# Streaming the attention prologue: normalising and projecting chunk by chunk inside the attention loop, with row statistics moved beside the residual adds

## The chip, the cores and the metric

The kernel runs on 1 core of one Trainium2 chip. The metric is the device time of one execution in microseconds (us). Executions of one kernel on one chip lie within about 0.3% of each other; a time more than 1.5% above the fastest of the same kernel counts as slow and is left out of comparisons.

Engines are named as in the profile: PE is TensorE (matmul), PEld its weight loads, DVE is VectorE, ACT is ScalarE, POOL is GpSimd, SP is SyncE.

## The reference

A sequence of 2048 rows of 512 features goes through four layers: attention (A), gated MLP (B), A, B, each on a layer-normalised copy and added back to the residual.

```python
def _A_ref(x, wq, wk, wv, wo):            # 32 heads of 16, one shared K and V
    q = (x @ wq).reshape(B, S, H, Dh).transpose(0, 2, 1, 3)
    k = x @ wk
    v = x @ wv
    p = softmax(einsum('bhqd,bkd->bhqk', q, k) * Dh ** -0.5)
    return einsum('bhqk,bkd->bhqd', p, v).transpose(0, 2, 1, 3).reshape(B, S, H * Dh) @ wo

def _B_ref(x, w_in, w_sp, b_sp, w_out):
    z = gelu(x @ w_in)
    z1, z2 = z[..., :Fh], layernorm(z[..., Fh:])
    g = einsum('ts,bsf->btf', w_sp, z2) + b_sp[None, :, None]
    return (z1 * g) @ w_out

x = x + A(layernorm(x)); x = x + B(layernorm(x))
x = x + A(layernorm(x)); x = x + B(layernorm(x))
```

## The kernel before

The kernel emits one instruction stream per engine; `K.op(engine, fn, waits, inc)` appends an operation with the semaphore values it waits for. Each stream is executed in the order in which it was appended, so a wait at its head holds up everything behind it (DVE's 5.32 us of idle time before L235, in the timeline of layer 0 below, is such a wait).

Every layer begins with this normalisation of all 16 row tiles (128 rows each):

```python
def layer_norm_T(lst, x_waits, extra_pe_waits):
    for t in range(NT):                                   # 16 statistics
        v = K.op("dve", ... e.bn_stats(ln_stats[:, t, :], X[:, t, :]), waits=x_waits, inc=S_dloc)
    v_stats = v
    for t in range(NT):
        v = K.op("dve", ... e.bn_aggr(ln_mv[:, t, :], ln_stats[:, t:t + 1, :]), waits=[(S_dloc, v_stats)], inc=S_dve)
    v1 = K.op("act", ... e.activation(ln_veps[:], ln_mv[:, :, 1], ACTF.Sqrt, bias=eps_c[:, 0:1]), ...)
    v_rstd_v = K.op("dve", ... e.reciprocal(ln_rstd[:], ln_veps[:]), waits=[(S_act, v1)], inc=S_dve)
    for t in range(NT):
        v = K.op("dve", ... e.tensor_scalar(xn[:, t, :], X[:, t, :], mean, rstd, subtract, mult), ...)
    # ... 8 groups: PE transposes two tiles into a PSUM bank, DVE copies them to xnT
```

Attention then makes K for all 4 chunks of 512 rows, V for all, and two of the 32 (chunk, head group) blocks of Q, and only then starts its loop:

```python
kT_ready = (S_dve, v_k_last)        # all of K
V_ready = (S_dve, v_v_last)         # all of V
...
emit_fill(0); emit_fill(1)          # scores of 3 blocks each, into PSUM
for i in range(NI):                 # 683 turns
    emit_exp(i)                     # ACT: exponential of 128 x 1536
    for u in pending_pv.get(i, []):
        emit_pv(u)                  # PE: probabilities times V
        emit_acc(u)                 # DVE: accumulate out of PSUM
    if i + 2 < NI:
        emit_fill(i + 2)            # PE: scores for two turns later; waits for exponential i
    emit_side_pe(allow_bg=(i % SIDE_PERIOD == 0))   # one "side task" on PE: Q block, ...
    emit_side_dve()                                 # and its copy on DVE
```

Side tasks share one PSUM bank (bank 7); each waits until the copy of the task before has emptied it. The six banks of scores, one of the accumulation and this one are the eight PSUM banks that the kernel addresses.

The softmax here doesn't subtract the row's maximum and nothing guards it: scores larger than these inputs give would overflow.

## Time and profile before

| | before |
|---|---|
| median of the first 5 executions | 2643.57 us (2641.64 to 2651.72) |
| ACT busy | 79% of the span |
| first exponential of layer 0 | 58.2 us |
| last residual add of layer 1 to first exponential of layer 2 | 36.1 us |

From the page of the kernel before: the busy line of all engines, then two rows of the 40 equal slices of the span (a digit is a tenth of busy time, or of the full TensorE clock), then the group of the exponentials with its count, busy time, mean ns and idle time.

```profile
PE 1924.7 (73%) x11232; PEld 541.8 (20%) x11232; DVE 1219.6 (46%) x2035; ACT 2081.7 (79%) x1653; POOL 0.7 (0%) x7
...
ACT  1999999999999999272029999999999999973800
...
PEclk9985555555555555698989555555555555557899
...
L669 ACT ACTIVATE P_ring<-ps_all 128x1536 bf16<-128x1536 f32 (+1 forms) x1366 | 1907.2, 1450 | 124.2 <-PE ps_all L650 92.3
```

ACT is at 9 in the two attention layers and below that only around the layer changes. The clock row says 5 (half of full speed) in most of attention.

From the timeline of the same run, the prologue of layer 0 (start, duration, engine, line, operation; in brackets the idle time before it and what ended it):

```profile
19.92 1.09 DVE L235 TENSOR_SCALAR w_out_r<-w_out_r 128x3584 bf16<-128x3584 bf16 x1 [5.32 <-DMA w_out_r<-in_B_w_out_dram]
...
22.74 8.97 DVE L254 BATCH_NORM_STATS2 ln_stats<-X 128x6 f32<-128x512 bf16 x15
31.75 1.17 DVE L258 BATCH_NORM_AGGREGATE ln_mv<-ln_stats 128x2 f32<-128x6 f32 x16
32.95 0.31 ACT L261 ACTIVATE ln_veps<-ln_mv,eps_c 128x16 f32<-128x16 f32 x1 [30.94 <-DVE ln_mv L258]
...
33.29 0.25 DVE L263 RECIPROCAL ln_rstd<-ln_veps 128x16 f32<-128x16 f32 x1 [0.37 <-ACT ln_veps L261]
33.58 5.25 DVE L267 TENSOR_SCALAR xn<-X,ln_mv,ln_rstd 128x512 bf16<-128x512 bf16 x16
...
45.87 3.73 PE L332 MATMUL ps_all<-xnT,wk_rep 128*128 128x512 bf16 x16 [0.79 <-DVE xnT L293]
...
58.20 2.79 ACT L669 ACTIVATE P_ring<-ps_all 128x1536 bf16<-128x1536 f32 x2 [23.64 <-PE ps_all L650]
```

All of this is serial: 16 statistics until 31.7 us, aggregation, the square root on ACT and reciprocal on DVE, 16 normalises, transposes, K, V, Q. ACT waits 23.6 us for the first scores. From the timeline around the change from layer 1 to layer 2:

```profile
1332.77 0.69 DVE L968 TENSOR_TENSOR X<-ps_all,X 128x512 bf16<-128x512 f32 x1 [0.82 <-PE ps_all L962]
1333.50 9.59 DVE L254 BATCH_NORM_STATS2 ln_stats<-X 128x6 f32<-128x512 bf16 x16
1343.12 1.17 DVE L258 BATCH_NORM_AGGREGATE ln_mv<-ln_stats 128x2 f32<-128x6 f32 x16
...
1369.58 2.79 ACT L669 ACTIVATE P_ring<-ps_all 128x1536 bf16<-128x1536 f32 x2 [23.65 <-PE ps_all L650]
```

Last residual add, 9.6 us of statistics, and the first exponential 36.1 us after the add ended (1369.58 - 1333.46).

The windows view of a stretch in the middle of attention (length, then busy us and instruction count for each engine, then the granted clock):

```profile
core 0: us, PE busy (x) PEld busy (x) DVE busy (x) ACT busy (x) POOL busy (x), PEclk, DMA share, GB/s
398.00:458.00 60.00, 43.63 (x262) 9.13 (x258) 23.29 (x36) 58.37 (x43) 0.00 (x0) 0.50 0.00 1
```

### The profile page before, as it was taken

What the parts mean: (1) busy time and instruction counts of PE and PEld (TensorE: products, weight loads), DVE (VectorE), ACT (ScalarE), POOL (GpSimd) and SP (SyncE); (2) the same over time, 40 slices, a digit from 0 to 9 for tenths busy, and PEclk for the clock granted to TensorE, in tenths of its full rate; (3) what the DMA queues carried; (4) which work ended last, traced back from release to release, by engine and by line L of the source; (5) the groups of instructions that cost most, each with busy time, mean ns of one, the idle gap of its engine ahead of it and who ended that gap; (6) DMA issues with size and microseconds to landing.
All of it is one profiled execution on the core that took longest, in us unless ns stands there. A gap on an engine that the chain in (4) does not pass through costs nothing.

```text
span 2642.8 us, 29476 instructions
## 1 busy us (share of the span) xinstructions
PE 1924.7 (73%) x11232; PEld 541.8 (20%) x11232; DVE 1219.6 (46%) x2035; ACT 2081.7 (79%) x1653; POOL 0.7 (0%) x7
## 2 busy tenths in 40 slices
PE   3888777777777777568968777777777777765699
PEld 2232111111111111223432111111111111112144
DVE  5655433343334333792366334333433343339733
ACT  1999999999999999272029999999999999973800
POOL 0000000000000000000000000000000000000000
PEclk9985555555555555698989555555555555557899
DMA  3053000000000000201000000000000000001020
GB/s 114 1 139 101 1 0 1 0 1 1 1 1 1 1 1 1 64 0 32 32 1 1 0 1 1 0 1 0 1 1 1 1 1 1 1 1 64 0 67 30
DMA packets 60042, 44.00 MB, mean 17 GB/s; under 512 B 34816, under 2 KB 57216, under 8 KB 59904
## 3 DMA queue, kind: packets, MB, share of 16 engines
q1 hardware_dynamic: 59904, 42.11, 5.4%
q8 instruction: 92, 1.51, 0.2%
q14 instruction: 46, 0.38, 0.0%
HBM read 31.62 MB, written 10.49 MB: 16 GB/s over the span
## 4 chain that ended last, share of the span: by engine, by line
PE 42%; DVE 27%; ACT 23%; issue 7%; DMA 0%; SPq 0%; ACTq 0%
ACT P_ring L669 21%; PE ps_all L684 21%; DVE acc_sb L707 13%; PE ps_all L930 7%; PE ps_all L650 7%; DVE ybuf L832 2%; PE ps_all L962 2%; PE ps_all L613 2%; DVE st L858 2%; DVE ln_stats L254 1%; DVE z2n L853 1%; DVE oT_bf L709 1%; ACT z2n L886 1%; DVE z1c L853 1%; PE ps_all L561 1%
## 5 line engine op out<-in xcount | busy, mean ns | idle before, releaser
L669 ACT ACTIVATE P_ring<-ps_all 128x1536 bf16<-128x1536 f32 (+1 forms) x1366 | 1907.2, 1450 | 124.2 <-PE ps_all L650 92.3
L707 DVE TENSOR_TENSOR acc_sb<-ps_all,acc_sb 128x512 f32<-128x512 f32 x896 | 618.4, 690 | 928.3 <-PE ps_all L684 926.8
L684 PE MATMUL ps_all<-P_ring,V_aug 128*32 128x512 bf16 x4096 | 600.7, 574 | 472.4 <-ACT P_ring L669 257.4
L650 PE MATMUL ps_all<-qT_pad,kT_rep 32*128 32x512 bf16 x4096 | 783.7, 572 | 25.0 <-ACT P_ring L669 12.1
L684 PEld LDWEIGHTS ps_all<-P_ring,V_aug 128*32 128x32 bf16 x4096 | 129.3, 100 | 937.5 <-ACT P_ring L669 914.1
L650 PEld LDWEIGHTS ps_all<-qT_pad,kT_rep 32*128 32x128 bf16 x4096 | 141.3, 97 | 584.4 <-issue 421.3
L930 PE MATMUL ps_all<-wspT,z2n 128*128 128x512 bf16 x896 | 209.1, 390 | 24.3 <-ACT z2n L886 24.3
L261 ACT ACTIVATE ln_veps<-ln_mv,eps_c 128x16 f32<-128x16 f32 x4 | 1.2, 308 | 223.1 <-DVE ln_mv L258 223.1
L930 PEld LDWEIGHTS ps_all<-wspT,z2n 128*128 128x128 bf16 x896 | 88.3, 99 | 144.1 <-ACT z2n L886 27.5
L843 ACT ACTIVATE thbuf<-ybuf 128x448 bf16<-128x448 f32 (+1 forms) x120 | 72.2, 601 | 55.0 <-DVE ybuf L832 51.0
L940 DVE TENSOR_TENSOR gtmp<-ps_all,bsp_bc 128x512 f32<-128x512 f32 x56 | 38.7, 692 | 151.0 <-PE ps_all L930 151.0
L785 PE MATMUL ps_all<-w_in_r,xnT 128*128 128x448 bf16 x256 | 67.0, 394 | 44.7 <-DVE z2n L853 42.8
L283 PE MATMUL ps_all<-ident,xn 128*128 128x128 bf16 x256 | 29.6, 310 | 86.7 <-DVE xn L267 73.4
L823 ACT ACTIVATE ybuf<-ps_all 128x448 f32<-128x448 f32 (+1 forms) x120 | 66.3, 553 | 28.1 <-PE ps_all L785 27.6
L832 DVE SCALAR_TENSOR_TENSOR ybuf<-ybuf,ps_all 128x448 f32<-128x448 f32 (+1 forms) x120 | 75.4, 628 | 3.5 <-ACT ybuf L823 3.2
L709 DVE TENSOR_TENSOR oT_bf<-ps_all,acc_sb 128x512 bf16<-128x512 f32 x64 | 44.2, 691 | 70.4 <-PE ps_all L684 70.3
L790 PE MATMUL ps_all<-xnT,w_in_r 128*128 128x512 bf16 x224 | 62.6, 408 | 10.8 <-DVE z1c L853 9.3
L408 DVE CAST qT_pad<-ps_all 128x512 bf16<-128x512 f32 x60 | 41.5, 692 | 50.6 <-PE ps_all L403 50.6
L403 PE MATMUL ps_all<-xnT,wq_pad 128*128 128x512 bf16 x240 | 62.2, 382 | 0.3 <-DVE o_norm L571 0.3
L962 PE MATMUL ps_all<-w_out_r,hT 128*128 128x512 bf16 x224 | 49.7, 379 | 12.1 <-DVE hT L946 12.1
L613 PE MATMUL ps_all<-wo_r,onT 128*128 128x512 bf16 x128 | 44.7, 486 | 10.2 <-DVE X L618 6.6
L561 PE MATMUL ps_all<-ident,oT_bf 128*128 128x128 bf16 x256 | 37.7, 299 | 19.5 <-DVE oT_bf L709 19.5
(62 smaller groups left out, 726.7 us busy)
## 6 DMA issues: line engine op xcount, KB each, us to landing
wspT<-wspt_scratch SPq DMA_DIRECT2D x8, 2048.0 KB, 8.2
wsp_stage<-in_B_w_sp_dram SPq DMA_DIRECT2D x16, 512.0 KB, 3.9
wspt_scratch<-wspT_tile SPq DMA_DIRECT2D x16, 512.0 KB, 5.0
X<-in_A_x_dram SPq DMA_DIRECT2D x1, 2048.0 KB, 8.4
out_dram<-X SPq DMA_DIRECT2D x16, 128.0 KB, 3.4
w_in_r<-in_B_w_in_dram SPq DMA_DIRECT2D x1, 1792.0 KB, 9.4
w_out_r<-in_B_w_out_dram SPq DMA_DIRECT2D x1, 896.0 KB, 10.6
wq_nat<-in_A_wq_dram SPq DMA_DIRECT2D x1, 512.0 KB, 9.5
```

What stands on the lines that cost most here:

```text
L613: ins = e.matmul(side_bank32[:, 0:D], onT[:, par, c, qt * 128:(qt + 1) * 128], wo_r[:, c, :], start=(c == 0), stop=(c == 3))
L650: ins = e.matmul(bk[:, 0:QC], kT_rep[32 * j:32 * j + 32, kt * 128:(kt + 1) * 128], qT_pad[32 * j:32 * j + 32, hg, qc * QC:(qc + 1) * QC], ...
L669: return e.activation(P_ring[:, s0:s0 + n, :], bank32(b0, n).rearrange("p (k q) -> p k q", k=n)[:, :, 0:QC], ACTF.Exp, scale=DH ** -0.5)
L684: ins = e.matmul(pv_bank[32 * j:32 * j + 32, 0:QC], V_aug[:, kt, 32 * j:32 * j + 32], P_ring[:, slot, :], tile_position=(0, 32 * j), start ...
L707: fn = lambda e: e.tensor_tensor(acc_sb[:], pv_bank[:, 0:QC], acc_sb[:], ALU.add)
L709: fn = lambda e: e.tensor_tensor(oT_bf[:, par, :], pv_bank[:, 0:QC], acc_sb[:], ALU.add)
L785: ins = e.matmul(bk[:, 0:448], xnT[:, kd, t * 128:(t + 1) * 128], w_in_r[:, kd, FH + h * 448:FH + (h + 1) * 448], start=(kd == 0), stop=(k ...
L823: st["a0"][k] = K.op("act", lambda e, slot=slot, bk=bk, n=n: e.activation(ybuf[:, slot, 0:n], bk[:, 0:n], ACTF.Square, scale=SQA), waits=w ...
L832: st["d3"][k] = K.op("dve", lambda e, slot=slot, bk=bk, n=n: e.scalar_tensor_tensor(ybuf[:, slot, 0:n], ybuf[:, slot, 0:n], GELU_C, bk[:, ...
L843: st["a1"][k] = K.op("act", lambda e, slot=slot, n=n: e.activation(thbuf[:, slot, 0:n], ybuf[:, slot, 0:n], ACTF.Tanh), waits=wl, inc=S_act)
L930: ins = e.matmul(bk[:, 0:TCW], z2n[:, sti, ft * 128:(ft + 1) * 128], wspT[:, wb, sti, :], start=(sti == 0), stop=(sti == NT - 1))
L962: ins = e.matmul(bk[:, 0:D], hT2[:, ft, tt * 128:(tt + 1) * 128], w_out_r[:, ft, :], start=(ft == 0), stop=(ft == NF1 - 1))
```

## The change

The intent is to let the exponentials start sooner. Three things are done:

1. The row statistics (`bn_stats`) leave the head of each layer. Each tile's are computed just after its residual add: in attention by DVE in a turn of the loop that has nothing urgent, in layer 1's output beside the matmuls of the next tile.
2. Attention normalises, transposes and projects only chunk 0 of 4 ahead of its loop. Chunks 1 to 3 become urgent side tasks (normalise, two transpose groups, K, V each). The scores of a key tile wait only for their own chunk.
3. The reciprocal root of the attention layers moves from ACT and DVE to POOL (add, then power -0.5), and 10 (layer 0) or 18 (layer 2) dummy matmuls on PE run meanwhile, the "warm-up" matmuls (`pe_warm` in the code). They are meant to bring PE to its full clock.

```diff
+    def ln_rstd_tiles(t0, n, v_mv):
+        v1 = K.op("pool", lambda e: e.tensor_scalar(ln_veps[:, t0:t0 + n], ln_mv[:, t0:t0 + n, 1], LN_EPS, None, op0=ALU.add),
+                  waits=[(S_dve, v_mv)], inc=S_ploc)
+        v2 = K.op("pool", lambda e: e.tensor_tensor(ln_rstd[:, t0:t0 + n], ln_veps[:, t0:t0 + n],
+                                                     mhalf[:, 0:1].to_broadcast([P, n]), ALU.pow),
+                  waits=[(S_ploc, v1)], inc=S_pool)
...
     def layer_norm_T(lst, x_waits, extra_pe_waits):
-            v = K.op("dve", lambda e, t=t: e.bn_stats(ln_stats[:, t, :], X[:, t, :]),
-                     waits=list(x_waits) + [(S_dloc, None)], inc=S_dloc)
...
     def layer_A(layer_idx, x_waits, do_wspt=False):
-        xn, xnT, xnT_v = layer_norm_T(lst, x_waits, extra_pe_waits=[])
-        xnT_all = (S_dve, max(xnT_v))
+        if layer_idx == 0:
+            for t in range(NT):
+                v_st = K.op("dve", lambda e, t=t: e.bn_stats(ln_stats[:, t, :], X[:, t, :]), waits=list(x_waits), inc=S_dloc)
+        for t in range(NT):
+            v_mv = K.op("dve", lambda e, t=t: e.bn_aggr(ln_mv[:, t, :], ln_stats[:, t:t + 1, :]), ...)
+        rstd_w = ln_rstd_tiles(0, NT, v_mv)
+        def pe_warm(e, n=10 if layer_idx == 0 else 18):
+            for _ in range(n):
+                ins = e.matmul(bank32(3)[:, 0:512], ident[:], wo_r[:, 0, :], start=True, stop=True)
+            return ins
+        K.op("pe", pe_warm, ...)
+        v_x0, _ = ln_direct_chunk(0, x_waits, xn, XR, xnT, [0, 1], bfree, rstd_w=rstd_w)
...  # K, V of chunk 0 and two Q blocks only
+        for c in range(1, NCH):
+            t_lns = make_lns_task(c)
+            side_urgent.append(t_lns)
+            for half in range(nh):
+                side_urgent.append(make_lnt_task(c, half))
+            side_urgent.append(make_k_task(c))
+            side_urgent.append(make_v_task(c))
...
         def emit_fill(i):
-                while (qc, hg) not in qT_ready:
+                kc = kt // CT
+                while (qc, hg) not in qT_ready or kc not in kT_ready:
                     progressed = emit_side_pe()
...
             emit_side_dve()
+            if st_pending and not side_urgent and i % 8 == 5:
+                emit_stat()
...
     # layer_B, after each residual add
+                if layer_idx == 1:
+                    vx = K.op("dve", lambda e, t=t: e.bn_stats(ln_stats[:, t, :], X[:, t, :]), waits=[(S_dve, vx)], inc=S_dve)
```

## The prediction

> **What bounds it now.** Two attention layers and two gated-MLP layers run in turn. In attention the exponential on ScalarE sets the pace: in 60 us windows ScalarE is busy 58 to 59.5 us, one 128x1536 exponential each 1.36 us (33.73 us for 25, granted clock 1.0) to 1.43 us (30.14 us for 21, clock 0.5). The change leaves that alone. Serial prologues stand between the layers (timeline view):
> - layer 0: row statistics end at 31.7 us, first exponential 58.2;
> - layer 2: last residual add ends 1333.5, first exponential 1369.6: 36 us;
> - layers 1 and 3: 9.6 us of statistics each (1070.1 and 2377.4), VectorE alone.
>
> **Removed from the critical path** (durations of the trace, scheduled by hand)
> - Statistics move beside the residual adds: in attention into VectorE slack (23 of 60 us busy), in the MLP output beside 1.5 us of matmuls per tile. Only the last tile's 0.65 us stays: 9.0 us saved in each of layers 1 and 3 and in layer 2.
> - Only chunk 0 of 4 is normalised, transposed and projected before attention. From aggregation start to first exponential: 1.2 aggregation + about 1 reciprocal root on GpSimd (estimate from its 0.1 to 0.3 us operations plus handoffs) + 0.7 + 0.7 slack for the warm-up matmuls + 2.7 transposes and copies + 3.9 K, V, Q0, Q1 on TensorE + 0.75 last copy + 0.5 scores = 11.6 us. Layer 0's first exponential comes near 43.3 us: 15 saved. Layer 2: 36.1 becomes about 12.3: 24 saved, its statistics included.
> - Sum: 15 + 24 + 18 = 57 us.
>
> **Added on the path.** Chunks 1 to 3 (12 normalises of 0.33, 6 transposes groups of 0.95, 3 K and 3 V of 0.9 to 1.07, and a 0.4 to 0.7 us copy each) go into the first 16 or so exponentials of each attention. There VectorE and TensorE each need about 1.5 us per exponential, against 1.36. Worse, the scores of key tile 4, 8, 12 wait for their chunk's transpose, copy, K, copy chain on in-order queues. By hand: a stall of about 2.5 us before exponential 5, 1 to 1.5 at the next two boundaries, 0.3 to 0.5 at some others: 7 us per attention, 14 in all. Statistics delaying an accumulation: about 1 us.
>
> **The warm-up matmuls** (10 and 18). The Trainium skill, "TensorE: Matmul & The Clock Gate", Part 1, says that the idle array runs at half clock until some 3.4 us of activity. The trace agrees in layer 2 (granted clock 0.50 from 1337 to 1353 us, then 1.00), but shows 1.00 throughout layer 0's prologue, and transposes cost 0.115 us at either. I expect under 2 us from them, of either sign.
>
> **Prediction: 57 - 15 = 42 us less: 2602 us** (-1.6%), 80% range 2588 to 2616. Chances: over 2% faster 0.13, within 2% 0.86, over 2% slower 0.01.
>
> **What would show it.** First exponential at 42 to 45 us; in layer 2 about 12 us after the last residual add; the MLP layers go from last residual add to aggregation in under 1 us; in the first 25 us of each attention ScalarE idles some 7 us, released by the scores, most before its sixth exponential; the steady attention at 1.43 us as before, with granted clock 0.5.
>
> **What would make it wrong.** GpSimd's power taking several us (it is on both attention prologues); stalls of the streamed chunks hiding (gain up to 52) or a cold array doubling them (gain under 30); moved statistics delaying accumulation at each tile; a different clock in attention, where 0.07 us per exponential over 1366 would be 100 us.

## The result, and the profile after

The changed kernel takes 2608.18 us (median of 9 executions, 2603.18 to 2963.03), the kernel before 2643.57 us (15 executions). The ratio of fast runs is 0.9859, with a 95% interval of 0.9846 to 0.9872: 1.4% faster, within the 2% band that counts as the same. Ratios are the mean time of one kernel's fast runs over that of the other's in the same rounds, so they are not quite the ratio of the medians quoted.

The execution that was profiled first took 2963 us, in the slow state. Its trace holds no clock record at all, and the profile prints a clock of 1.00 for it. Its matmuls tell another story. From the timeline of its layer 0:

```profile
32.19 4.83 PE L400 MATMUL ps_all<-wo_r,ident 128*128 128x512 bf16 x10 [32.19 <-DVE ln_stats L392]
...
40.17 1.95 PE L411 MATMUL ps_all<-xnTA,wk_rep 128*128 128x512 bf16 x4 [0.79 <-DVE xnTA L287]
```

Ten 128x512 matmuls in 4.83 us, and the K of one chunk (4 matmuls) in 1.95 us, where before had 16 such in 3.73 us including waits: here it ran at about half clock. The mean 128x512 matmul of layer B's largest group took 674 ns against 390 before. It was not at one low clock throughout, though: in steady attention (exponentials 171 to 341 of layer 0) the median score matmul took 506 ns, between the 602 ns of the second profile below (granted clock 0.50 there) and the 384 ns of e11 (1.00). It is not compared further. All readings of "after" below are from a second profile of the same kernel (2604.76 us median of 4 executions on its chip, ratio 0.9858).

The lines of the page that answer to those of before:

```profile
PE 1905.3 (73%) x11198; PEld 538.0 (21%) x11260; DVE 1220.9 (47%) x2033; ACT 2081.1 (80%) x1650; POOL 7.1 (0%) x11
...
ACT  2999999999999999373049999999999999974800
...
PEclk9986555555555555698999655555555555557899
...
L809 ACT ACTIVATE P_ring<-ps_all 128x1536 bf16<-128x1536 f32 (+1 forms) x1366 | 1908.8, 1451 | 272.5 <-PE ps_all L790 242.5
```

ACT's idle time before exponentials is not to be compared as it stands: ACT no longer does a square root in the gap between layers 1 and 2, so the gap of 139.1 us, which `before` books under that root, is now booked under the exponentials. The timeline of layer 0's prologue:

```profile
31.91 1.17 DVE L394 BATCH_NORM_AGGREGATE ln_mv<-ln_stats 128x2 f32<-128x6 f32 x16
...
32.02 4.22 PE L400 MATMUL ps_all<-wo_r,ident 128*128 128x512 bf16 x10 [32.02 <-DVE ln_stats L392]
...
33.17 0.26 POOL L258 TENSOR_SCALAR ln_veps<-ln_mv 128x16 f32<-128x16 f32 x1 [31.66 <-DVE ln_mv L394]
...
33.51 2.93 POOL L260 TENSOR_TENSOR ln_rstd<-ln_veps,mhalf 128x16 f32<-128x16 f32 x1
...
36.48 1.38 DVE L268 TENSOR_SCALAR xnA<-X,ln_mv,ln_rstd 128x512 bf16<-128x512 bf16 x4 [3.40 <-POOL ln_rstd L260]
...
45.84 2.79 ACT L809 ACTIVATE P_ring<-ps_all 128x1536 bf16<-128x1536 f32 x2 [43.85 <-PE ps_all L790]
```

First exponential at 45.8 us instead of 58.2. The reciprocal root is the longest item: 0.26 us of add and 2.93 us of power on POOL, 3.40 us with the handoffs, where before had 0.66. Then the change from layer 1 to layer 2:

```profile
1319.67 0.69 DVE L1122 BATCH_NORM_STATS2 ln_stats<-X 128x6 f32<-128x512 bf16 x1
1320.40 1.17 DVE L394 BATCH_NORM_AGGREGATE ln_mv<-ln_stats 128x2 f32<-128x6 f32 x16
...
1332.69 2.79 ACT L809 ACTIVATE P_ring<-ps_all 128x1536 bf16<-128x1536 f32 x2 [139.06 <-PE ps_all L790]
```

From the end of the last residual add (1319.64) to the first exponential: 13.1 us instead of 36.1. And the change from layer 0 to layer 1, last residual add, one statistic, aggregation:

```profile
1064.29 0.69 DVE L755 TENSOR_TENSOR X<-ps_all,X 128x512 bf16<-128x512 f32 x1 [1.25 <-PE ps_all L750]
1065.01 0.69 DVE L560 BATCH_NORM_STATS2 ln_stats<-X 128x6 f32<-128x512 bf16 x1
1065.74 1.17 DVE L318 BATCH_NORM_AGGREGATE ln_mv<-ln_stats 128x2 f32<-128x6 f32 x16
```

Only one tile's statistics are left between add and aggregation, 0.76 us instead of 9.66. Last, the new stall of the streamed chunks, before exponential 5 (counting from 0) of layer 0:

```profile
51.24 1.03 PE L279 MATMUL ps_all<-ident,xnA 128*128 128x128 bf16 x8
...
52.31 0.69 DVE L287 COPY xnTA<-ps_all 128x1024 bf16<-128x1024 bf16 x1 [0.77 <-PE ps_all L279]
...
53.06 1.04 PE L411 MATMUL ps_all<-xnTA,wk_rep 128*128 128x512 bf16 x3 [0.24 <-DVE xnTA L287]
54.13 0.69 DVE L416 CAST kT_rep<-ps_all 128x512 bf16<-128x512 f32 x1 [0.53 <-PE ps_all L411]
...
54.88 0.39 PE L790 MATMUL ps_all<-qT_pad,kT_rep 32*128 32x512 bf16 x3 [0.79 <-DVE kT_rep L416]
...
55.32 2.79 ACT L809 ACTIVATE P_ring<-ps_all 128x1536 bf16<-128x1536 f32 x2 [2.52 <-PE ps_all L790]
```

Transpose, copy, K, copy, scores: each waits for the one before, on in-order queues, and ACT idles 2.52 us at the end of it.

The gain, place by place, from the starts of the same operations in the two traces:

| place | before, us | after, us | gain, us |
|---|---|---|---|
| layer 0: first exponential | 58.20 | 45.84 | 12.4 |
| layer 0: first exponential to end of the last | 994.1 | 1001.4 | -7.3 |
| layer 1: last add of layer 0 to aggregation | 9.66 | 0.76 | 8.9 |
| layer 2: last add of layer 1 to first exponential | 36.1 | 13.1 | 23.1 |
| layer 2: first exponential to end of the last | 990.0 | 997.0 | -7.0 |
| layer 3: last add of layer 2 to aggregation | 9.66 | 0.76 | 8.9 |
| rest of layers 1 and 3 | | | -0.9 |
| sum | | | 38.1 |

In both attention layers, 6.1 of the 7 us given back are lost in the first 32 exponentials; the rest of attention has nearly the same intervals, turn by turn, as before.

### The profile page after: what moved, and what is told of

It is laid out like the page before. It is cut to its first block, busy times and chain, and to the rows that moved or that the text cites. A ratio compares the mean times of both kernels' runs of the same rounds, so it can differ in the third digit from the quotient of the medians.

```text
span 2961.1 us, 29539 instructions
## 1 busy us (share of the span) xinstructions
PE 2269.8 (77%) x11260; PEld 603.8 (20%) x11260; DVE 1225.2 (41%) x2033; ACT 2059.4 (70%) x1650; POOL 7.1 (0%) x11
## 4 chain that ended last, share of the span: by engine, by line
PE 57%; DVE 21%; ACT 16%; issue 5%; DMA 0%; SPq 0%; POOL 0%; ACTq 0%
PE ps_all L829 19%; ACT P_ring L809 15%; PE ps_all L1080 14%; DVE acc_sb L852 12%; PE ps_all L790 7%; PE ps_all L513 4%; PE ps_all L940 4%; PE ps_all L1112 4%; PE ps_all L750 2%; DVE st L1008 1%; DVE oT_bf L854 1%; ACT z2n L1036 1%; DVE z2n L1003 1%; DVE ybuf L982 1%; PE ps_all L698 1%
## 5 line engine op out<-in xcount | busy, mean ns | idle before, releaser
L809 ACT ACTIVATE P_ring<-ps_all 128x1536 bf16<-128x1536 f32 (+1 forms) x1366 | 1884.3, 1452 | 483.5 <-PE ps_all L790 475.3
L829 PE MATMUL ps_all<-P_ring,V_aug 128*32 128x512 bf16 x4096 | 576.2, 555 | 523.2 <-ACT P_ring L809 260.0
L790 PE MATMUL ps_all<-qT_pad,kT_rep 32*128 32x512 bf16 x4096 | 706.1, 521 | 26.6 <-DVE kT_rep L416 3.3
L1080 PE MATMUL ps_all<-wspT,z2n 128*128 128x512 bf16 x896 | 421.9, 674 | 25.1 <-ACT z2n L1036 25.1
L1080 PEld LDWEIGHTS ps_all<-wspT,z2n 128*128 128x128 bf16 x896 | 132.0, 148 | 314.2 <-issue 286.4
L513 PE MATMUL ps_all<-xnTA,wq_pad 128*128 128x512 bf16 x240 | 117.1, 649 | 0.7 <-DVE o_norm L708 0.7
L1112 PE MATMUL ps_all<-w_out_r,hT 128*128 128x512 bf16 x224 | 104.6, 674 | 12.1 <-DVE hT L1096 12.1
L935 PE MATMUL ps_all<-w_in_r,xnT 128*128 128x448 bf16 x256 | 106.9, 567 | 8.8 <-DVE z2n L1003 6.3
L940 PE MATMUL ps_all<-xnT,w_in_r 128*128 128x512 bf16 x224 | 104.8, 678 | 0.6 <-DVE z2n L1003 0.6
L698 PE MATMUL ps_all<-ident,oT_bf 128*128 128x128 bf16 x256 | 32.5, 275 | 24.8 <-DVE oT_bf L854 24.8
L1112 PEld LDWEIGHTS ps_all<-w_out_r,hT 128*128 128x128 bf16 x224 | 32.3, 147 | 84.4 <-issue 63.7
```

Of the source, the lines that this page charges most:

```text
L513: ins = e.matmul(side_bank32[:, 0:QC], wq_pad[:, kd, hg, :], xnT[:, kd, qc * QC:(qc + 1) * QC], start=(kd == 0), stop=(kd == KD - 1))
L790: ins = e.matmul(bk[:, 0:QC], kT_rep[32 * j:32 * j + 32, kt * 128:(kt + 1) * 128], qT_pad[32 * j:32 * j + 32, hg, qc * QC:(qc + 1) * QC], ...
L809: return e.activation(P_ring[:, s0:s0 + n, :], bank32(b0, n).rearrange("p (k q) -> p k q", k=n)[:, :, 0:QC], ACTF.Exp, scale=DH ** -0.5)
L829: ins = e.matmul(pv_bank[32 * j:32 * j + 32, 0:QC], V_aug[:, kt, 32 * j:32 * j + 32], P_ring[:, slot, :], tile_position=(0, 32 * j), start ...
L935: ins = e.matmul(bk[:, 0:448], xnT[:, kd, t * 128:(t + 1) * 128], w_in_r[:, kd, FH + h * 448:FH + (h + 1) * 448], start=(kd == 0), stop=(k ...
L940: ins = e.matmul(bk[:, 0:TCW], w_in_r[:, kd, ft * 128:(ft + 1) * 128], xnT[:, kd, tc * TCW:(tc + 1) * TCW], start=(kd == 0), stop=(kd == K ...
```

## The experiments

Four kernels ran on one chip with a kernel before of 2643.15 us, four on another with 2649.09, four on a third with 2641.35. All twelve gave correct results. The first of them (e1) is the changed kernel itself, whose profile has just been shown.

> The changed kernel again, unaltered, because its profile on record fell in a slow execution. Expected: about 2608 us in the fast state. In the profile: first exponential of layer 0 near 46 us (the slow profile had 49.1 with cold matmuls; aggregation ends 33.2, the root on GpSimd takes 0.26 + 2.93 us instead of the 1 us in the prediction), layer 2's first exponential 14 to 15 us after its last residual add. Theory A (the shortfall of 37 measured against 42 predicted is GpSimd's power, 2 x 2.4 us): exponential stalls in the first 25 us of each attention sum to about 7 us. Rival B (the shortfall is the streamed chunks): those stalls sum to 10 us or more per attention. Rival C (the moved statistics delay accumulations): steady attention per head group is longer than the 30.63 us of before.

**Measured.** 2604.76 us, ratio 0.9858 (0.9844 to 0.9871). First exponential of layer 0 at 45.8, of layer 2 13.1 us after the add. ACT's idle time before exponentials 1 to 17 sums to 5.1 us in each attention. Rival B wanted 10 or more, theory A about 7. Theory A's account of the shortfall, two slow roots, is taken up under e5: it holds only in part. Rival C, longer head groups everywhere, does not hold: apart from one spot near exponential 512 (+1.4 and +1.8 us) and stretches in layer 0 where the clock changes, the intervals are those of before.

### e2: the statistics alone

```diff
# on the kernel before
-            v = K.op("dve", ... e.bn_stats(ln_stats[:, t, :], X[:, t, :]) ...)   # head of layers 1, 2, 3
+            # emit_stat() in attention and bn_stats after layer 1's residual adds, as in the change
```

> The kernel before with only the row statistics moved beside the residual adds. Theory A: the statistics leave the critical path whole, all but the last tile's: 3 x 9.0 = 27 us less than before, near 2617 us (ratio 0.990). Rival C (the moved statistics delay accumulations in attention or the residual chain of the MLP): 20 us or less.

**Measured.** 2619.0 us, ratio 0.9908 (0.9894 to 0.9923): 24 us less than before. Last residual add to aggregation is 0.76 us in all three places, so 3 x 8.9 = 26.7 us left the path as expected; 1 to 4 us were lost again inside attention. That is nearer to theory A (27) than to rival C (20 or less), though the interval of the ratio, 20 to 28 us, does not separate the two; the trace does.

### e3: the streaming alone

```diff
# on the changed kernel
-        if layer_idx == 0:
+        if True:                      # statistics at the head of every attention layer
...                                    # and of every MLP layer; emit_stat() and layer 1's bn_stats removed
```

> The changed kernel with the statistics back at the head of each layer: streaming, GpSimd root and warm-up matmuls alone. Theory A: 37 - 27 = 10 us less than before, near 2634 us (ratio 0.996): two first exponentials about 12 us earlier each, less about 7 us of stalls each. If the two parts are not additive (rival D: the statistics gain only because the prologue was shortened), this one plus the statistics-only run fall short of or exceed 37 us by more than 5.

**Measured.** 2632.22 us, ratio 0.9956 (0.9942 to 0.9971): 10.9 us less than before. With e2's 24.2 that makes 35.1, against 38.4 for the whole change on this chip. The parts are additive within the 5 us that rival D was given. About two thirds of the gain is the statistics; the elaborate streaming brings the smaller share. (In layer 2 of e3 the first 17 exponentials took 3.5 us longer than in e1, with more of them at half clock: see the table under e5.) At exponential 512 this run shows +0.1 and +0.6 us where e1 and e2, with moved statistics, have +1.4 to +2.2, so the moved statistics do cost about 1 us per attention.

### e5: the root back on ACT and DVE

```diff
-        v1 = K.op("pool", ... tensor_scalar(..., LN_EPS, None, op0=ALU.add)); v2 = K.op("pool", ... ALU.pow)
+        v1 = K.op("act", ... e.activation(ln_veps, ln_mv[:, t0:t0 + n, 1], ACTF.Sqrt, bias=eps_c[:, 0:1]), ...)
+        v2 = K.op("dve", ... e.reciprocal(ln_rstd, ln_veps), waits=[(S_act, v1)], inc=S_dve)
```

This is the root as before. (A version with add and power in one DVE instruction did not compile.)

> The changed kernel with the reciprocal root of the attention layers done as before (ScalarE square root, VectorE reciprocal: 0.66 us from aggregation to normalising in the trace of before) in place of GpSimd's add and power (3.4 us in the slow trace). Theory A: 2 x 2.7 = 5.5 us less than the changed kernel, near 2602 us, unless the warm-up matmuls (4 us from the end of the statistics) then hold up the first transposes, in which case 2 to 4 us. Rival B: within 1 us of the changed kernel.

**Measured.** 2607.49 us, ratio 0.9869 (0.9855 to 0.9883): no gain. The first exponentials do come 2.4 us (layer 0) and 1.5 us (layer 2, from the last add) earlier than in e1, but the advantage is gone by exponential 11. Its timeline shows where:

```profile
31.90 4.42 PE L398 MATMUL ps_all<-wo_r,ident 128*128 128x512 bf16 x10 [31.90 <-DVE ln_stats L390]
...
32.99 0.31 ACT L258 ACTIVATE ln_veps<-ln_mv,eps_c 128x16 f32<-128x16 f32 x1 [30.98 <-DVE ln_mv L392]
...
33.62 1.38 DVE L266 TENSOR_SCALAR xnA<-X,ln_mv,ln_rstd 128x512 bf16<-128x512 bf16 x4
...
36.12 1.54 PE L277 MATMUL ps_all<-ident,xnA 128*128 128x128 bf16 x16
...
43.45 6.85 ACT L807 ACTIVATE P_ring<-ps_all 128x1536 bf16<-128x1536 f32 x5 [8.85 <-PE ps_all L788]
...
50.55 1.03 PE L409 MATMUL ps_all<-xnTA,wk_rep 128*128 128x512 bf16 x2 [0.24 <-DVE xnTA L285]
...
51.80 0.63 PE L409 MATMUL ps_all<-xnTA,wk_rep 128*128 128x512 bf16 x1 [0.22 <-issue]
...
53.88 1.45 ACT L807 ACTIVATE P_ring<-ps_all 128x1536 bf16<-128x1536 f32 x1 [3.58 <-PE ps_all L788]
```

Two things have to be told apart. First, the root itself is worth less than 2.4 us. The normalises start 2.9 us earlier than in e1 (33.62 against 36.48), but the first transposes only 1.15 (36.12 against 37.27): they wait behind the warm-up matmuls, which run to about 36.3 (ends of matmuls are modelled), as the expectation had allowed for. And the prologue of layer 0 held 3.4 us of half clock in e1, but none that is on record in e5. From the start of aggregation to the first exponential it took 13.9 us in e1, 12.3 in e6 and e11 (the same prologue without that stretch) and 11.7 in e5. So in layer 0 the root is worth 0.65 us and the clock 1.6; in layer 2, where neither has half clock in the prologue, the root is worth 1.5.

Second, what was gained is lost in the loop. The K of chunk 1 (PE at 50.55 and 51.80) is slower than the same in e1, and exponential 5 has an idle time of 3.58 us before it instead of 2.52. Its windows show why:

```profile
core 0: us, PE busy (x) PEld busy (x) DVE busy (x) ACT busy (x) POOL busy (x), PEclk, DMA share, GB/s
46.00:50.00 4.00, 3.69 (x34) 1.74 (x34) 2.23 (x4) 4.00 (x4) 0.00 (x0) 0.67 0.00 0
50.00:54.00 4.00, 2.76 (x13) 0.78 (x11) 1.78 (x3) 0.42 (x2) 0.00 (x0) 0.50 0.02 4
54.00:58.00 4.00, 3.73 (x31) 2.19 (x29) 2.31 (x6) 3.09 (x3) 0.00 (x0) 0.50 0.00 0
```

The granted clock fell to half from about 47 to 61 us. In e1 it was at half for only one stretch of 3.4 us in this part. So a new theory, E: the length of the streamed part hangs on the clock that PE happens to have there. The traces of all kernels that keep this order of tasks, later ones included, one entry for each attention, sorted by the half-clock time between exponentials 0 and 17:

| run, layer | half clock, us | exponentials 0 to 17, us |
|---|---|---|
| before, 0 and 2 (nothing streamed) | 0 | 22.9, 22.9 |
| e6, 0 and 2; e9, 0 and 2 | 0 | 28.0 to 28.1 |
| e1, 0 and 2; e3, 0; e8, 2; e4, 0; e11, 0 and 2 | 3.4 | 29.0 to 29.2 |
| e8, 0; e5, 2 | 6.8 | 30.2, 30.1 |
| e5, 0; e4, 2 | 13.7 | 31.8, 31.8 |
| e3, 2 | 17.1 | 32.5 |

The tasks and their order are the same there (e6, e9 and e11 have dummy matmuls between them), and the time grows with the half-clock time throughout. (The slow execution, with no clock on record, took 38.2 in both.)

### e4: no warm-up matmuls

```diff
-        K.op("pe", pe_warm, ...)
```

> The changed kernel without its two groups of warm-up matmuls. Theory E (granted clock decides how long the streamed part takes: in the two traces of the changed kernel and of its square-root variant the streamed part lasted 27.3 us with one half-clock stretch of some 3 us and 30.2 us with one of 14 us): without them the K, V and Q matmuls before the first exponential run at half clock (0.43 us instead of 0.22 us each), first exponential 2 to 3 us later in each attention, and the streamed part no shorter: 3 to 8 us slower than the changed kernel. Rival F: they change nothing, within 1.5 us, because the idle time that GpSimd's 2.93 us power leaves after them lets the clock drop anyway.

**Measured.** 2611.39 us, ratio 0.9856 (0.9839 to 0.9874), the same ratio as the changed kernel on its chip. The trace is not so even: the first exponential is 1.1 us later in layer 0 and 2.4 us later in layer 2 (from the last add) than in e1, and layer 2's first 17 exponentials take 31.8 us at 13.7 us of half clock. That is 6.5 us worse up to there, as theory E says. (Against e6 and e11, without half clock in the prologue, layer 0's prologue is 2.9 us longer. Its 128x128 transposes start every 107 ns, those of e6 every 56.) But layer 0 between exponentials 24 and 171, where Q blocks and transposes of the spatial weight come as side tasks, took 206.9 us at 66.8 us of half clock, against 212.2 at 100.0 in e1 and 216.8 at 127.3 in e9. This clock history differs from run to run for reasons that the runs do not show, and it hides the rest. What the warm-up matmuls are worth in the total is left open; it is not more than the interval, some 5 us.

### e6: dummy matmuls where PE idles

```diff
         emit_fill(0)
         if NI > 1:
             emit_fill(1)
+        K.op("pe", pe_hold)                          # 5 dummy 128x512 matmuls
...
+            if i == 0:
+                K.op("pe", lambda e: pe_hold(e, 4))  # 4 more after the third score group
```

> The changed kernel with 5 dummy 128x512 matmuls after the first two score groups and 4 after the third, where TensorE idles before the first exponential is done. If the half-clock stretch in the streamed part comes from that idle time (theory E), the granted clock stays 1.00 through the first 17 exponentials, and they take 1 to 2 us less than the 27.3 us of the changed kernel, each attention: 2 to 4 us less in all. If the stretch is not of that cause, no gain or a loss of up to 1 us.

**Measured.** 2606.43 us where before had 2649.09, ratio 0.9835 (0.9816 to 0.9854). In the trace, no half-clock time in the streamed part of either attention, 28.05 us instead of 28.95 in both, as expected. The ratio leaves open whether the total gains (its interval overlaps that of e1), but the cause of the half-clock stretch, PE's idle time around the first exponentials, is shown: of the eight attentions with dummy matmuls there (e6, e9, e10, e12) seven have no half clock in the first 17 exponentials, and all 14 streamed attentions without them (e1, e3, e4, e5, e7, e8, e11) have 3.4 us or more.

### e7: the streamed tasks begin one turn earlier

```diff
         emit_fill(0)
         if NI > 1:
             emit_fill(1)
+        emit_side_pe()      # normalise chunk 1
+        emit_side_pe()      # its first transposes
+        emit_side_dve()     # their copy
```

> The changed kernel with the first two streamed tasks (normalise, first transposes of chunk 1) issued before the loop instead of in its first two turns, so that the K of chunk 1 is ready earlier. My prediction put a stall of 2.5 us before exponential 5 on the in-order chain transpose, copy, transpose, copy, K, copy; the trace shows 2.52 us of idle ScalarE there. If that chain is the cause: that stall falls under 0.7 us in both attentions, and the kernel gains 3 to 5 us. If the streamed part is bound by the sum of VectorE or TensorE work (rival), the stall reappears at the later chunks and the gain is under 1.5 us.

**Measured.** 2603.51 us (before 2649.09), ratio 0.9826 (0.9809 to 0.9844). The timeline lines of the exponentials around the first chunk boundary of layer 0:

```profile
45.55 6.85 ACT L809 ACTIVATE P_ring<-ps_all 128x1536 bf16<-128x1536 f32 x5 [43.55 <-PE ps_all L790]
...
52.81 2.79 ACT L809 ACTIVATE P_ring<-ps_all 128x1536 bf16<-128x1536 f32 x2 [0.40 <-PE ps_all L790]
```

The stall before exponential 5 falls from 2.52 to 0.40 us. Part of it comes back: idle times of 0.3, 0.8 and 0.8 us before exponentials 7, 8 and 9, where e1 had 0.0, 0.1 and 0.0. The first 17 exponentials take 27.25 instead of 28.95 us in each attention, at the same 3.4 us of half clock. The dependent chain is the cause of the largest stall (1.7 us gained of 2.5); what remains, 4.4 us over the 22.9 of before, is not from that chain. About 1.2 of it goes with the 3.4 us of half clock (26.0 us without any in layer 2 of e10, which has the same head start); the rest is spread over the later turns, in which PE and DVE work through the tasks.

### e8: layer 0's statistics before the weight layout

```diff
         v0 = dve_memset(wq_pad[:], 0.0)
+        for t in range(NT):
+            v_st0 = K.op("dve", ... e.bn_stats(ln_stats[:, t, :], X[:, t, :]), waits=[(S_x, S_x.n)], inc=S_dloc)
...
-        K.op("dve", ... e.tensor_scalar(w_out_r[:], w_out_r[:], 0.5, None, op0=ALU.mult), waits=[wB], ...)
+        # the same, after layer 0's prologue
```

> The changed kernel with layer 0's statistics started as soon as its input has landed, ahead of the weight layout, and the scaling of the output weights put off to after the prologue. In the trace VectorE idles from 3 to 12.8 and from 14.6 to 19.9 us waiting for weights. Expected: aggregation starts at about 21.5 us instead of 31.9, the kernel gains 9 to 11 us. If the statistics in layer 0 are not on the critical path: no gain.

**Measured.** 2598.32 us (before 2649.09), ratio 0.9809 (0.9792 to 0.9826). Aggregation starts at 21.6 us instead of 31.9, the first exponential at 33.9 instead of 45.8, and the trace ends 9.4 us earlier than that of e1. In layer 0, DVE's statistics were waiting behind weight layout and a scaling that waited for weight loads (9.78 us idle before 12.83 us, and 5.32 before the line at 19.92 in the timeline of before), although their own input had landed: in e8 they start at 9.18 us. The two moves, statistics forward and scaling back, were not tried apart.

### e9: the root on ACT, with the clock held by dummy matmuls

```diff
# e5 and e6 together
```

> The changed kernel with the ScalarE square root (which alone gained nothing: its streamed part took 31.8 and 30.1 us at 13.7 and 6.8 us of half clock, against 29.0 at 3.4) and with the filler matmuls that kept the clock at 1.00 there. Theory E (the clock ate the root's gain): the first exponentials come 2.4 and 1.5 us earlier than in the changed kernel and the first 17 exponentials now take about 28.1 us, as with the fillers alone: about 4 us less than the filler run, ratio near 0.982. Rival G (whatever makes the prologue shorter is lost in the streamed part, since TensorE and VectorE work there is the bound): the streamed part is again 30 us or more although the clock stays at 1.00.

**Measured.** 2600.83 us, ratio 0.9844 (0.9831 to 0.9858). In the trace theory E is confirmed against rival G: no half clock, and 28.05 and 28.04 us for the first 17 exponentials. Exponential 16 of layer 0 comes at 70.0 us instead of e1's 73.2, but most of that is the clock: in e6, with the fillers and GpSimd's root, it comes at 70.6. Against e6 the root is worth 0.6 us in layer 0 and 1.5 in layer 2 up to there, half of the 4 us that I had expected. In the total the expected 0.982 is missed; the profiled execution ended at 2606.6 us, because its layer 0 then spent 127 us at half clock between exponentials 24 and 171 and took 4.6 us longer there than e1. The executions of this kernel spread from 2596 to 2608 us. So the root's gain is real in the prologue, but small, and not resolved in the total.

### e10: what gained, together

```diff
# e7, e8, the root of e5, and 3 dummy matmuls after the first two score groups
```

> All that gained, together: early statistics in layer 0 (10.3 us earlier aggregation in its trace), head start of the streamed tasks (first 17 exponentials 27.25 against 28.95 us), ScalarE root, and 3 filler matmuls after the first two score groups. Expected: first exponential of layer 0 near 32 us, first 17 exponentials 26 to 27 us in both attentions with the clock at 1.00, 15 to 20 us less than the changed kernel: near 2588 us, ratio 0.979. If the parts eat each other through the clock, over 2595 us.

**Measured.** 2591.59 us (before 2641.35), ratio 0.9811 (0.9798 to 0.9825). First exponential of layer 0 at 33.2 us; first 17 exponentials 27.95 us (with 3.4 us of half clock) in layer 0 and 26.03 (none) in layer 2. Better than the changed kernel by 0.5%, where I had expected 0.7%. But e8 alone had reached 0.9809: by the ratios, what was added to it here shows no gain. (The times themselves are from two chips, whose kernel before differs by 7.7 us. Both intervals lie on both sides of 0.98, so neither run counts as over 2% faster.) In the trace of e10, layer 0 spent 127 us at half clock between exponentials 24 and 171 and took 216.2 us there, 3.4 more than in e8, about what its first 17 exponentials had gained.

### e11: the clock held through all of attention

```diff
             emit_side_pe(allow_bg=(i % SIDE_PERIOD == 0))
             emit_side_dve()
+            if len(side_emitted) == held and side_state["k_dve"] == held:   # no side task in this turn
+                K.op("pe", pe_keep, waits=[(S_sdve, sdve_base + held)])     # 2 dummy 128x512 matmuls
```

> The changed kernel with two dummy 128x512 matmuls in each turn of the attention loop that has no side task of its own. My prediction said that the clock in attention is worth 0.07 us per exponential. If so, the granted clock stays 1.00 through attention, an exponential takes 1.36 us instead of 1.43, and the kernel loses some 80 to 95 us: near 2520 us, ratio 0.953. Rival H: at half clock the exponentials are paced by ScalarE itself, or the extra matmuls delay the scores: within 10 us of the changed kernel or slower.

**Measured.** 2484.83 us, ratio 0.9410 (0.9397 to 0.9423): 5.9% faster than before, though PE does 2304 useless matmuls more. Its page and a window in the middle of attention:

```profile
PE 2080.5 (84%) x13564; PEld 622.4 (25%) x13564; DVE 1219.1 (49%) x2033; ACT 2019.9 (81%) x1650; POOL 7.1 (0%) x11
...
PEclk9999999999999999798999999999999999989799
```

```profile
core 0: us, PE busy (x) PEld busy (x) DVE busy (x) ACT busy (x) POOL busy (x), PEclk, DMA share, GB/s
398.00:458.00 60.00, 51.89 (x363) 13.19 (x363) 24.13 (x38) 60.00 (x46) 0.00 (x0) 1.00 0.00 1
```

The clock row is at 9 where it was at 5, ACT has no idle time in the window, and from exponential 171 to 341 of layer 0 an exponential comes every 1.354 us (230.2 us for 170) instead of 1.464 (248.9 in e1). The two attention layers together, from first to last exponential, take 1880 us instead of e1's 1998: 118 us, which is the difference between the ratios 0.9858 and 0.9410 too. (The first part of each attention was at full clock for some time already, so the 0.11 us does not count for all 1366.) My estimate of 0.07 us per exponential was too small: the half-clock figure in it (21 exponentials in 30.14 us) was read from a stretch inside one head group, without the stalls at half clock between groups. The dummy matmuls are not free: in exponentials 24 to 60 of layer 0, where e1 has full clock anyway, e11 takes 3.9 us longer.

### e12: both

```diff
# e10 and e11 together
```

> The combination run and the held clock together. If the two are independent: the sum of both gains, near 2500 us, ratio 0.945. If the held clock fails, within 10 us of the combination run.

**Measured.** 2464.91 us, ratio 0.9334 (0.9321 to 0.9347). It beats both kernels by more than 5%. The two gains add up: 2641.35 - 2591.59 = 49.8 and 2641.35 - 2484.83 = 156.5 us, less the changed kernel's own gain of some 37 us that is counted in both (1 - 0.9858 of 2641), make 169; measured are 176.4.

## Why the prediction was right

It said 2602 us (2588 to 2616), within 2% of before. Measured are 2608.18 us, 35 us less than before by the medians (37 by the ratio of fast runs, 38.1 between the two traces) instead of 42. The traces leave 3.9 us to explain.

- **Statistics off the path: right.** 9.0 us in each of three places was predicted; last add to aggregation fell by 8.9 us, and e2 alone gained 24.
- **First exponentials: right in mechanism, one term mis-sized.** Layer 0's was predicted near 43.3 us and came at 45.8; layer 2's about 12 us after the last add, and came 13.1 after it. The mis-sized term is "about 1 reciprocal root on GpSimd (estimate from its 0.1 to 0.3 us operations plus handoffs)". It measured 3.40 us: the power alone takes 2.93 us for a 128x16 operand. Scaling from memsets said nothing about a power. The Trainium skill, "Perfetto Trace Analysis", section "Optimizing GPSIMD Operations", says to prefer other engines where possible, and here the trace agrees: 0.66 us on ACT and DVE against 3.40. The prediction named this as the first thing that could go wrong. But the two terms, 2.4 us each too small, are not 4.8 us of shortfall: the 0.7 us of slack that I had allowed for the warm-up matmuls was not needed, since the power outlasts them, and with the root back on ACT and DVE the warm-up matmuls hold up the transposes instead (e5). What the slow root cost is 0.65 us in layer 0 and 1.5 in layer 2. Layer 0 lost 1.6 us more to half clock in its prologue, which was in no term.
- **Stalls of the streamed chunks: right in mechanism, the size with some luck.** Predicted were 7 us per attention, 2.5 of them before exponential 5. The traces show 6.1 us lost in the first 32 exponentials and 2.52 us there; e7 confirms the dependent chain as its cause. About 0.9 of the 6.1, and 0.8 of the 2.52, is the stretch of half clock (e6), which the sum did not have; in e3 and e5, with more of it, up to 9.6 us are lost.
- **Statistics delaying accumulations, about 1 us: about right**, but per attention instead of in all (e2 and e3 against e1, at exponential 512).
- **Warm-up matmuls under 2 us either way: not settled.** The totals of e4 and e1 agree, the traces show 6.5 us that later clock changes made up for. The reading behind it was wrong in one point: I wrote that the trace "shows 1.00 throughout layer 0's prologue". The trace of before has no clock record ahead of 45.7 us; the profile prints 1.00 where there is none. In e1 the ten warm-up matmuls took 0.42 us each in a part printed as 1.00. So "transposes cost 0.115 us at either" compares half clock with half clock: in before they start every 107 ns in both prologues, in e6, with granted clock 1.00 on record, every 56.
- **Steady attention as before at half clock: right** for the change (0.50 and 58.4 of 60 us of ACT in the same window of both). What the clock is worth there was mis-sized: 0.11 us per exponential, not 0.07.

The step that nobody had in the sum is the clock in the streamed part: between none and 17.1 us at half clock, the same tasks take 28.0 to 32.5 us. It is why the earlier first exponentials of e5 were lost again before exponential 11.

## What to carry to other kernels

Before splitting a serial prologue into streamed pieces, take what can simply be moved: here the statistics beside the residual adds gave 24 of 38 us, and an in-order queue that held ready statistics behind late weight loads held some 10 more. When a piece on the path is made faster and the total does not move, look at what else fills the wait (here the warm-up matmuls) and at the granted clock after it; a shorter wait can be spent on slower matmuls. A printed clock of 1.00 is no reading where the trace has no clock record. And when the profile shows a half clock through a long steady stretch, ask first what that costs the engine that sets the pace: two useless matmuls per turn were worth 118 us, three times the whole change.

## What the Trainium skill lacked or had wrong

- "TensorE: Matmul & The Clock Gate", section "Why this matters for your kernels", advises to keep TensorE busy with no gaps over about 3 us to stay at full clock. In the steady attention of before the longest idle gap of PE between 398 and 518 us is 1.1 us and PE is busy 43.6 of 60 us, and the granted clock is 0.50 for hundreds of us. Two more 128x512 matmuls of full height per turn (e11, busy 51.9 of 60) make it 1.00. The attention's own matmuls use 32 rows or 32 columns of the array; whether the threshold lies in that or in the busy share was not separated. The page's "A second HAM failure mode: psum-queue depth-cycling" does tell of short idles between matmul groups that make the clock oscillate, but no section says how the busy share and the part of the array count.
- The same page, Part 4, says that transpose mode does not count as busy in the same way and that the full clock does not engage for it. In layer 2 of before the clock went from 0.50 to 1.00 at 1356.4 us, after transposes alone (busy 1.89 and 5.51 us from 1345.8 on) and before K's first matmul (1357.25 us); in layer 2 of e2 it went up at 1337.8 us, again before K (1339.99). These are the kernel's `e.transpose`, which the trace prints as MATMUL.
- The same page, "Seeing it yourself", warns that clock (HAM) records are unreliable, but not that a whole slow execution can pass without any: 2963 us against 2608, with a printed clock of 1.00, and ten 128x512 matmuls in 4.83 us. In the fast traces the first record comes only 26 to 46 us into the span.
- "GPSIMD Engine Reference", section 3.1 (elementwise), gives cycles per element and a time for an add, and no page has a time for a power. A power on 128x16 float32 takes 2.93 us, a tensor_scalar add of the same shape 0.26 us.
